# Four column tiles of 32 instead of two of 64 for the main products of a polysketch-attention and ELU kernel

## The chip, the core and the metric

The kernel runs on one core of a Trainium2 chip. The metric is the device time of one execution in microseconds (us). A core has a matrix engine (TensorE, PE in the profile, with its weight loads as PEld), a vector engine (VectorE, DVE), a scalar engine (ScalarE, ACT), GpSimd (POOL) and SyncE (SP), which here only issues DMAs. All arithmetic is float32.

## The reference

Polynomial-sketch attention over 4 batches, 4 heads, 1088 positions and head size 32 gives a matrix of 4352 tokens by 128; two dense layers with an ELU between them follow. The second part does nearly all the arithmetic.

```python
def phi(x):                              # r = 8, so 64 features
    a = np.einsum('rd,bhsd->bhsr', S1, x)
    b = np.einsum('rd,bhsd->bhsr', S2, x)
    return np.einsum('bhsi,bhsj->bhsij', a, b).reshape(*x.shape[:-1], r * r)
q_p, k_p = phi(q), phi(k)
kv  = np.einsum('bhsf,bhsd->bhfd', k_p, v);   z = np.sum(k_p, axis=2)
num = np.einsum('bhsf,bhfd->bhsd', q_p, kv)
den = np.einsum('bhsf,bhf->bhs', q_p, z)[..., None] + 1e-06
x   = (num / den).transpose(0, 2, 1, 3).reshape(4352, 128)
h   = x @ w_in                           # w_in 128 x 2048
g   = np.where(h > 0, h, np.exp(np.minimum(h, 0)) - 1)
out = g @ w_out                          # w_out 2048 x 128
```

## The kernel before

The tokens are cut into nine groups of the queries: groups 0 to 7 hold 512 tokens each, group 8 holds 256. The hidden size of 2048 is cut into eight pairs (`cp` = 0 to 7) of two 128-wide chunks (`c` = 0, 1). A step is one group and one pair, so there are 72 steps, listed in `steps`. All instructions are placed by hand in program order (a manual schedule). The main loop at the end of the kernel does, for step n: the first layer of step n (`mm1`), extra attention work that `at`, `mid` and `late` have hung on this step, the ELU of step n, and the second layer of step n-2.

- `mm1` computes h = w_in^T x for both chunks of the pair. `mm1_first` does the same for the very first step, with 256 columns at a time.
- The ELU is two ACT passes (lines 787 and 789) and one DVE pass (line 795, which writes the tile `gg`).
- The second layer has three forms. Groups 0 and 1 use `mm2`. Groups 2 to 7 use `mm2_seven`: the product of a pair with w_out is written as seven products of half size in the manner of Strassen, whose operand sums `tt` are made by POOL (lines 706 to 711) and whose weight sums are the tile `SS`. Group 8 uses `mm2_last`, with the hidden values as the stationary operand.
- Attention for the next groups runs between these. Per batch b, `KF` or `KF_late` makes the key features (line 303, line 322), `KA` (line 390, with `z_tile` on line 381) sums them with the values into `kv`, and `Z` and `KV` turn the sums by products with `SXh` and with an identity matrix. `q1` (line 538) and `q5` (line 644) make the query features and the attention output of a group. `q1_first`, `q1z_first`, `q1_second`, `q4_early` and `q5_early` do this for groups 0 and 1 in the prologue.

Every product with w_in and w_out and every turning product fills 128 output partitions from a contraction over 128 partitions. The stationary operand has 128 columns. The helper `halves` (line 225) cuts these into two column tiles of 64, each 128 partitions by 64 columns of the array, given by `tile_position`; `mm2_seven` (line 726) does it in its own loop, where the two tiles take the same 64 weight columns and different halves of the moving operand. Other products use other cuts: `KA` and `z_tile` use four column tiles of 128x32, `KF`, `q1_first`, `q1z_first` and `q1_second` two of 128x64, `KF_late` and `q5_early` tiles of 64x32, `q1` and `q5` tiles of 64x64 or 32x32. `keep_warm` and the transposes use the whole array. The profile prints the cut of a matrix instruction as rows*columns, for example 128*64.

One float32 matmul of the program shows in the trace as two weight loads (LDWEIGHTS) and two matmuls (MATMUL), called its two passes here.

Of the kernel before, what the change touches and what calls it, by code (L numbers as in the profile page):

```python
# [27 lines left out]
def kernel(  # L28
# [21 lines left out]
    nc = tc.nc  # L50
    B, H, S, D = q.shape
    R = S1.shape[0]
    P = 128
# [95 lines left out]
    W = const.tile([P, NP, 4 * P], F32, name="W")  # L149
# [50 lines left out]
    ident = const.tile([P, P], F32, name="ident")  # L200
# [19 lines left out]
    idle = psum.tile([P, 512], F32, name="idle", tag="o0", bufs=1)  # L220


    def halves(dst, lhs, rhs, **kw):
        for u in range(2):
            nc.tensor.matmul(dst[64 * u:64 * u + 64], lhs[:, 64 * u:64 * u + 64], rhs, skip_group_check=True,  # L225
                             tile_position=(0, 64 * u), **kw)

    def keep_warm(n, cols=256):
        for i in range(n):
# [16 lines left out]
    SXh = const.tile([P, FD], F32, name="SXh")  # L246
# [46 lines left out]
    kv_ps, kvz, feats, wzs, kf_ps = {}, {}, {}, {}, []  # L293
# [111 lines left out]

    def Z(b, ps, zl):

        halves(ps[:, 96:128], SXh[:], zl[:])

    def Z_out(b, ps):  # L410
        z = wzs[b] = SW[:, :, 2, :] if b == 0 else work.tile([FD, H, R], F32, name="wz", tag="wz")[:]
# [7 lines left out]

    def KV(b, ps):  # L420
        for f in range(2):
            halves(ps[:, 128 + P * f:128 + P * f + P], kvz[b][:, f].rearrange("p c s -> p (c s)"), ident[:])

    def KV_out(b, ps):
        if b in kvs:
# [8 lines left out]
    def Z_first():  # L434
        ps = psum.tile([P, 512], F32, name="zps", tag="h", bufs=4)
        for i in range(KT):
            z_tile(0, ps, i)
        return ps, ZC(0, ps)
# [7 lines left out]
    def KV_first():  # L446
        ps = psum.tile([P, 512], F32, name="kvps", tag="aux")
        KV(0, ps)
        KV_out(0, ps)
# [5 lines left out]
    abw, ans, qp, qpT, xg, xps = {}, {}, {}, {}, {}, {}  # L455
# [224 lines left out]
    hs, es, gs, ops = {}, {}, {}, {}  # L680
# [16 lines left out]
    def quarter(g, cp, c, y):  # L697
        return gs[g, cp][:, c].rearrange("p (u x s) -> p u x s", u=2, x=2)[:, :, y, :]
# [14 lines left out]
    def mm2_seven(g, cp, first, last):  # L713
        if first:
            acc[g] = [psum.tile([P, 512], F32, name="pa", tag="o0", bufs=1),
                      psum.tile([P, 512], F32, name="pb", tag="o1", bufs=1)]
        a, b = acc[g]
        t, w = ts.pop((g, cp)), [W[:, cp, 2 * P + 64 * i:2 * P + 64 * i + 64] for i in range(4)]
        b11, b21, b22 = quarter(g, cp, 0, 0), quarter(g, cp, 1, 0), quarter(g, cp, 1, 1)
        p1, p2, p6 = (a, 0, w[0], b11), (a, 1, w[2], b21), (a, 2, SS[:, 1, cp], t[:, 1])  # L720
        p4, p5 = (b, 0, w[3], t[:, 3]), (b, 1, SS[:, 0, cp], t[:, 0])
        p7, p3 = (b, 2, SS[:, 2, cp], t[:, 2]), (b, 3, SS[:, 3, cp], b22)
        todo = [p1, p2, p6, p3, p5, p7, p4] if first or last else [p1, p2, p3, p5, p7, p6, p4]
        for i, (bank, col, lhs, rhs) in enumerate(todo):
            for u in range(2):
                nc.tensor.matmul(bank[64 * u:64 * u + 64, P * col:P * col + P], lhs, rhs[:, u],  # L726
                                 start=(first and i in (0, 3)), stop=last, skip_group_check=True,
                                 tile_position=(0, 64 * u))
        del gs[g, cp]

    def fin_seven_copy(g):
# [34 lines left out]
    def mm1(g, cp, cs=(0, 1)):  # L766
        n = qn[g] * P
        if 0 in cs and (g, cp) not in hs:
            hs[g, cp] = [psum.tile([P, 512], F32, name="h", tag="h", bufs=4) for c in range(2)]
        for c in cs:  # L770
            halves(hs[g, cp][c][:, :n], W[:, cp, c * P:c * P + P], xg[g][:, :n])

    def mm1_first():
        hs[0, 0] = [psum.tile([P, 512], F32, name="h", tag="h", bufs=4) for c in range(2)]
        for w in range(2):
            for c in range(2):
                cols = [x[:].rearrange("p (m w s) -> p w m s", w=2, s=P)[:, w] for x in (hs[0, 0][c], xg[0])]
                halves(cols[0], W[:, 0, c * P:c * P + P], cols[1])

    def elu_a(g, cp, c, parts=(0, 1)):  # L780

# [20 lines left out]
    def mm2(g, cp, first, last):  # L802
        n = qn[g] * P
        if first:
            ops[g] = psum.tile([P, 512], F32, name="o", tag=f"o{g % 2}", bufs=1)
        gg = gs.pop((g, cp))
        for c in range(2):
            halves(ops[g][:, :n], W[:, cp, (2 + c) * P:(3 + c) * P], gg[:, c, :n],
                   start=(first and c == 0), stop=(last and c == 1))

    def fin1(g):
# [12 lines left out]
    def mm2_last(cp, first, last):  # L824
        g = NQ - 1
        if first:
            ops[g] = [psum.tile([P, P], F32, name="ol", tag=t, bufs=k) for t, k in (("o0", 1), ("aux", 2))]
        gg = gs.pop((g, cp))
        for a in range(4):
            c, i = (a % 2, a // 2) if last else divmod(a, 2)  # L830
            halves(ops[g][i][:], gg[:, c, i * P:i * P + P], W[:, cp, (2 + c) * P:(3 + c) * P],
                   start=(first and c == 0), stop=(last and c == 1))

    def fin_last():
# [14 lines left out]
    zps, zl = Z_first()  # L849
    q1_first()  # L850
    KO_pool()
    KO_first(4, 5)
    KO_first(5, 7)
    Z(0, zps, zl)
    Z_out(0, zps)
    KO_first(7, KT)
# [14 lines left out]
    q5_early(0)  # L871
    q1_second()
    mm1_first()
    RA(2)
    RB(2)
    RC(1)
    elu_a(0, 0, 0)
    elu_a(0, 0, 1)
    mm1(0, 1)
    q2(1, 2)  # L880
    q4_early(1)
# [4 lines left out]
    elu_d(0, 0, 1)  # L886
    q5_early(1)
    mm2(0, 0, True, False)
    RC(3)
    for c in range(2):  # L890
# [40 lines left out]
    def turn(b):  # L931
        Z(b, kv_ps[b], zls.pop(b))
        KV(b, kv_ps[b])
# [59 lines left out]
    for n in range(2, N + 2):  # L993
        if n < N:
            g, cp = steps[n]
            mm1(g, cp)
        for f, *a in extra.get(n, ()):
            f(*a)
        if n < N:
            elu(g, cp, 0)  # L1000
            if seven(g):
                sums7(g, cp, 0)
            for f, *a in extra.get((n, 0), ()):
                f(*a)
            before = steps[n - 2]
            ends = n > 3 and seven(before[0]) and before[1] == NP - 1
            if ends:
                elu_a(g, cp, 1, (0,))
                mm2_seven(*before, False, True)
                fin_seven_copy(before[0])  # L1010
                elu_a(g, cp, 1, (1,))
                fin_seven_a(before[0])
                elu_d(g, cp, 1)
            else:
                elu(g, cp, 1)
            if seven(g):
                sums7(g, cp, 1)
            if ends:
                fin_seven_b(before[0])
        for f, *a in extra.get((n, 1), ()):  # L1020
            f(*a)
        g, cp = steps[n - 2]
        if g == NQ - 1:
            mm2_last(cp, cp == 0, cp == NP - 1)
        elif seven(g):
            if cp < NP - 1:
                mm2_seven(g, cp, cp == 0, False)
        elif n > 2:
            mm2(g, cp, cp == 0, cp == NP - 1)
            if cp == NP - 1:  # L1030
                fin1(g)
# [30 lines left out]
```

## Time and profile before

| | |
|---|---|
| median of 5 runs | 267.39 us (267.13 to 267.83) |
| the profiled execution: its own time | 267.83 us |
| the profiled execution: its span | 266.0 us |
| PE busy | 260.0 us, 3113 matmul records |
| PEld busy | 154.9 us, 3113 weight-load records |
| DVE / ACT / POOL busy | 187.9 / 184.1 / 159.9 us |
| granted TensorE clock | 1.00 in every window looked at |

How to read it: "L225" is line 225 of the kernel. A group row gives line, engine, operation, out<-in, the cut and the moving size, the number of records, then busy time and mean duration of one. Records of PE overlap each other, because matmuls are pipelined and because several tiles run at once. The pace of PE is therefore read from the times between starts, not from durations. A row of the timeline merges neighbouring records of one kind: start in us, extent from the first start to the last end in us, then what they are, and how many.

### The profile page before, as it was taken

The page shows a single profiled execution, that of the slowest core. Times are in us where ns is not written, and L with a number is a line of the kernel's source. Part 1 is how long each engine was busy: PE and PEld are TensorE (multiplying, and loading weights), DVE is VectorE, ACT ScalarE, POOL GpSimd, SP SyncE. Part 2 cuts the span into 40 slices and gives each one's busy share as a digit, 9 for nine tenths or more (in the row PEclk, how much of TensorE's full clock was granted, in tenths as well). Part 3 has the DMA queues.
Part 4 walks back from the last instruction along what each step waited for, and adds up shares of the span by engine and source line. Part 5 has one row for each costly group of instructions (what it writes and reads, how often), then busy time and mean ns, then how long its engine had stood idle before and what let it go on. Part 6 is the DMA issues. An engine that isn't in the chain of part 4 may idle for free.

```text
span 266.0 us, 7682 instructions
## 1 busy us (share of the span) xinstructions
PE 260.0 (98%) x3113; PEld 154.9 (58%) x3113; DVE 187.9 (71%) x347; ACT 184.1 (69%) x355; POOL 159.9 (60%) x233
## 2 busy tenths in 40 slices
PE   8899999999999999999999999999999999999994
PEld 7743323343334665668566666666766666667884
DVE  7799999996969796996657766554346444673652
ACT  2479978677566565786577777777777777777782
POOL 4400008203405985798858799898688888898300
PEclk9999999999999999999999999999999999999999
DMA  5998960011002300001100110001000100010011
GB/s 186 321 348 240 283 174 10 0 40 48 0 0 35 50 4 0 2 2 18 27 5 0 21 22 2 0 12 27 9 0 15 28 4 0 14 18 13 2 30 32
DMA packets 26402, 13.60 MB, mean 51 GB/s; under 512 B 19200, under 2 KB 24576, under 8 KB 26368
## 3 DMA queue, kind: packets, MB, share of 16 engines
q1 hardware_dynamic: 25920, 12.79, 18.7%
q8 instruction: 24, 0.39, 0.6%
q10 hardware_dynamic: 448, 0.33, 0.4%
q14 instruction: 10, 0.08, 0.1%
HBM read 10.88 MB, written 2.23 MB: 49 GB/s over the span
## 4 chain that ended last, share of the span: by engine, by line
PE 93%; DVE 5%; issue 1%; ACT 0%; DVEq 0%
PE h L225 43%; PE pb L726 16%; PE pa L726 12%; PE o L225 11%; PE ol L225 3%; PE kv L390 1%; PE idle L230 1%; PE h L644 1%; PE qps L644 1%; PE abp L303 1%; DVE qp L582 1%; PE kfps L322 1%; PE qps L538 1%; PE kv L225 1%; DVE raw L121 1%
## 5 line engine op out<-in xcount | busy, mean ns | idle before, releaser
L795 DVE SCALAR_TENSOR_TENSOR gg<-e,h 128x512 f32<-128x512 f32 (+1 forms) x144 | 92.2, 652 | 64.1 <-ACT e L789 62.8
L225 PE MATMUL h<-xg,W 128*64 128x512 f32 (+1 forms) x584 | 128.9, 563 | 0.0
L787 ACT ACTIVATE e<-h 128x512 f32<-128x512 f32 (+1 forms) x144 | 81.5, 566 | 50.5 <-PE h L225 46.7
L789 ACT ACTIVATE e<-e 128x512 f32<-128x512 f32 (+1 forms) x144 | 87.5, 607 | 4.4
L225 PEld LDWEIGHTS h<-xg,W 128*64 128x64 f32 x584 | 40.2, 137 | 47.4 <-issue 37.3
L706 POOL TENSOR_TENSOR tt<-gg 128x256 f32<-128x256 f32 x48 | 35.2, 733 | 16.3 <-DVE gg L795 15.9
L709 POOL TENSOR_TENSOR tt<-gg 128x256 f32<-128x256 f32 x48 | 35.5, 739 | 14.1 <-DVE gg L795 13.8
L711 POOL TENSOR_TENSOR tt<-gg,tt 128x256 f32<-128x256 f32 x48 | 36.6, 762 | 3.8
L710 POOL TENSOR_TENSOR tt<-tt,gg 128x256 f32<-128x256 f32 x48 | 35.2, 734 | 3.8
L726 PEld LDWEIGHTS pa<-gg,W 128*64 128x64 f32 x384 | 23.6, 137 | 22.8 <-issue 22.0
L225 PE MATMUL o<-gg,W 128*64 128x512 f32 x128 | 30.5, 597 | 0.4 <-DVE W L129 0.4
L726 PE MATMUL pa<-gg,W 128*64 128x128 f32 x384 | 29.5, 274 | 0.0
L726 PE MATMUL pb<-tt,SS 128*64 128x128 f32 x384 | 29.1, 273 | 0.0
L726 PEld LDWEIGHTS pb<-tt,SS 128*64 128x64 f32 x384 | 22.6, 137 | 0.0
L126 POOL TENSOR_TENSOR raw<-raw,tiny 128x512 f32<-128x512 f32 x1 | 1.0, 1042 | 30.0 <-DVE raw L121 30.0
L726 PE MATMUL pb<-gg,SS 128*64 128x128 f32 x192 | 18.7, 273 | 0.0
L726 PE MATMUL pb<-tt,W 128*64 128x128 f32 x192 | 18.6, 273 | 0.0
L726 PE MATMUL pa<-tt,SS 128*64 128x128 f32 x192 | 18.6, 273 | 0.0
L225 PEld LDWEIGHTS o<-gg,W 128*64 128x64 f32 x128 | 8.5, 136 | 16.2 <-issue 13.8
L726 PEld LDWEIGHTS pa<-tt,SS 128*64 128x64 f32 x192 | 12.1, 137 | 0.0
L726 PEld LDWEIGHTS pb<-tt,W 128*64 128x64 f32 x192 | 12.1, 137 | 0.0
L726 PEld LDWEIGHTS pb<-gg,SS 128*64 128x64 f32 x192 | 12.1, 137 | 0.0
(150 smaller groups left out, 244.6 us busy)
## 6 DMA issues: line engine op xcount, KB each, us to landing
raw<-in_moe_w_in_dram SPq DMA_DIRECT2D x8, 256.0 KB, 6.5
raw<-in_moe_w_out_dram SPq DMA_DIRECT2D x8, 256.0 KB, 6.6
hd_k<-in_k_dram SPq DMA_DIRECT2D x3, 544.0 KB, 8.0
hd_q<-in_q_dram SPq DMA_DIRECT2D x3, 544.0 KB, 8.2
v<-in_v_dram SPq DMA_DIRECT2D x4, 288.0 KB, 7.6
out_dram<-ob SPq DMA_DIRECT2D x72, 16.0 KB, 1.5
v<-in_v_dram SPq DMA_DIRECT2D x4, 256.0 KB, 6.9
out_dram<-ob SPq DMA_DIRECT2D x16, 32.0 KB, 1.6
```

What stands on the lines that cost most here:

```text
L121: nc.vector.scalar_tensor_tensor(lo.bitcast(F32), lo, 2.0 ** -32, raw[:, :, 1], op0=MUL, op1=ADD)
L225: nc.tensor.matmul(dst[64 * u:64 * u + 64], lhs[:, 64 * u:64 * u + 64], rhs, skip_group_check=True, tile_position=(0, 64 * u), **kw)
L230: nc.tensor.matmul(idle[:, :cols], some[:, :P], some[:, :cols], skip_group_check=True)
L644: nc.tensor.matmul(ps[w][s * r:s * r + s, 64 * k:64 * (k + m)], lhs, qpT[g, i][rows, o + 2 * k:o + 2 * (k + m), f, :], start=(f == 0 and j ...
L706: nc.gpsimd.tensor_tensor(t[:, 0], b12, b11, op=SUB)
L709: nc.gpsimd.tensor_tensor(t[:, 2], b22, b12, op=SUB)
L710: nc.gpsimd.tensor_tensor(t[:, 1], t[:, 2], b11, op=ADD)
L711: nc.gpsimd.tensor_tensor(t[:, 3], b21, t[:, 1], op=SUB)
L726: nc.tensor.matmul(bank[64 * u:64 * u + 64, P * col:P * col + P], lhs, rhs[:, u], start=(first and i in (0, 3)), stop=last, skip_group_che ...
L787: nc.scalar.activation(e, hs[g, cp][c][:, :n], RELU, scale=-1.0)
L789: nc.scalar.activation(e, e, EXP, scale=-1.0)
L795: nc.vector.scalar_tensor_tensor(gs[g, cp][:, c, :n], es[g, cp][:, c, :n], -1.0, hs[g, cp][c][:, :n], op0=ADD, op1=MAX)
```

## The change

`halves` becomes `quarters`: four matmuls, one for each column tile of 32. All six callers follow it (`Z`, `KV`, `mm1`, `mm1_first`, `mm2`, `mm2_last`). The loop of `mm2_seven` gains an inner loop, so that each of its half-width products is cut in two again. Nothing else is edited: the same values are multiplied, into the same banks, in the same order of products. In the changed kernel the line of `quarters` is again 225, and the matmul of `mm2_seven` is on line 728.

```diff
-    def halves(dst, lhs, rhs, **kw):
-        for u in range(2):
-            nc.tensor.matmul(dst[64 * u:64 * u + 64], lhs[:, 64 * u:64 * u + 64], rhs, skip_group_check=True,
-                             tile_position=(0, 64 * u), **kw)
+    def quarters(dst, lhs, rhs, **kw):
+        for c in range(4):
+            nc.tensor.matmul(dst[32 * c:32 * c + 32], lhs[:, 32 * c:32 * c + 32], rhs, skip_group_check=True,
+                             tile_position=(0, 32 * c), **kw)
...
     def Z(b, ps, zl):
-        halves(ps[:, 96:128], SXh[:], zl[:])
+        quarters(ps[:, 96:128], SXh[:], zl[:])
...
     def mm2_seven(g, cp, first, last):
...
             for u in range(2):
-                nc.tensor.matmul(bank[64 * u:64 * u + 64, P * col:P * col + P], lhs, rhs[:, u],
-                                 start=(first and i in (0, 3)), stop=last, skip_group_check=True,
-                                 tile_position=(0, 64 * u))
+                for w in range(2):
+                    r = 64 * u + 32 * w
+                    nc.tensor.matmul(bank[r:r + 32, P * col:P * col + P], lhs[:, 32 * w:32 * w + 32], rhs[:, u],
+                                     start=(first and i in (0, 3)), stop=last, skip_group_check=True,
+                                     tile_position=(0, r))
...
     def mm1(g, cp, cs=(0, 1)):
...
-            halves(hs[g, cp][c][:, :n], W[:, cp, c * P:c * P + P], xg[g][:, :n])
+            quarters(hs[g, cp][c][:, :n], W[:, cp, c * P:c * P + P], xg[g][:, :n])
```

`KV`, `mm1_first`, `mm2` and `mm2_last` change in the same way, by the name of the helper alone.

More of the change, by code (lines that the diff above doesn't have):

```diff
@@ L421, in KV @@
         for f in range(2):
-            halves(ps[:, 128 + P * f:128 + P * f + P], kvz[b][:, f].rearrange("p c s -> p (c s)"), ident[:])
+            quarters(ps[:, 128 + P * f:128 + P * f + P], kvz[b][:, f].rearrange("p c s -> p (c s)"), ident[:])
     def KV_out(b, ps):
@@ L777, in mm1_first @@
                 cols = [x[:].rearrange("p (m w s) -> p w m s", w=2, s=P)[:, w] for x in (hs[0, 0][c], xg[0])]
-                halves(cols[0], W[:, 0, c * P:c * P + P], cols[1])
+                quarters(cols[0], W[:, 0, c * P:c * P + P], cols[1])
     def elu_a(g, cp, c, parts=(0, 1)):
@@ L807, in mm2 @@
         for c in range(2):
-            halves(ops[g][:, :n], W[:, cp, (2 + c) * P:(3 + c) * P], gg[:, c, :n],
+            quarters(ops[g][:, :n], W[:, cp, (2 + c) * P:(3 + c) * P], gg[:, c, :n],
                    start=(first and c == 0), stop=(last and c == 1))
@@ L830, in mm2_last @@
             c, i = (a % 2, a // 2) if last else divmod(a, 2)
-            halves(ops[g][i][:], gg[:, c, i * P:i * P + P], W[:, cp, (2 + c) * P:(3 + c) * P],
+            quarters(ops[g][i][:], gg[:, c, i * P:i * P + P], W[:, cp, (2 + c) * P:(3 + c) * P],
                    start=(first and c == 0), stop=(last and c == 1))
```

## The prediction

> **What bounds the kernel now.** I read the page first: the busy row, the clock row, the queues and the chain that ended last.
>
> ```profile
> PE 260.0 (98%) x3113; PEld 154.9 (58%) x3113; DVE 187.9 (71%) x347; ACT 184.1 (69%) x355; POOL 159.9 (60%) x233
> ...
> PEclk9999999999999999999999999999999999999999
> ...
> q8 instruction: 24, 0.39, 0.6%
> ...
> PE 93%; DVE 5%; issue 1%; ACT 0%; DVEq 0%
> ```
>
> PE carries 93% of the chain, at full clock. Busy PE alone is no proof of a bound, so the second view is PE's timeline of one whole step with seven products, which gives the pace between starts.
>
> ```profile
> 200.85 0.61 PE L726 MATMUL pa<-gg,W 128*64 128x128 f32 x8
> 201.29 0.39 PE L726 MATMUL pa<-tt,SS 128*64 128x128 f32 x4
> 201.51 0.39 PE L726 MATMUL pb<-gg,SS 128*64 128x128 f32 x4
> 201.73 0.61 PE L726 MATMUL pb<-tt,SS 128*64 128x128 f32 x8
> 202.16 0.39 PE L726 MATMUL pb<-tt,W 128*64 128x128 f32 x4
> 202.38 1.89 PE L225 MATMUL h<-xg,W 128*64 128x512 f32 x8
> 204.10 0.61 PE L726 MATMUL pa<-gg,W 128*64 128x128 f32 x8
> ```
>
> From 200.85 to 202.38 there are 28 records of 128 columns in 1.53 us. They start in pairs, one for each column tile, so 14 pairs take 109 ns each. From 202.38 to 204.10 four pairs of 512 columns take 1.72 us, 430 ns each. Both fit 0.833 ns a column plus 2.5 ns. The next step begins with no gap. From 22.3 us to the last matmul at 262.4 us the matrix engine streams like this; what interrupts it is almost only a change of the tile cut. Thus the pace of a pass, and the price of a change of cut, are the two things by which this edit can move the end.
>
> **The change part by part.**
>
> *1. The passes.* A pass over all 128 output columns is now four records instead of two, each reading the same moving columns. From the records of the groups I count the old pairs: 316 of 512 columns (504 and 128 records), 40 of 256 (80), 848 of 128 (1536 of line 726, 128 of `mm2_last`, 32 of `KV`), 8 of 32; 1212 in all. Every nanosecond that a pass of four costs beyond a pass of two is 1.2 us. The trace holds the same form already: `KA` runs four 128*32 tiles at once. The clearest is batch 0, which starts behind a wait, with nothing queued.
>
> ```profile
> 10.19 1.21 PE L390 MATMUL kv<-kp,v 128*32 128x64 f32 x72
> ```
>
> A record here lasts 0.22 us, so the last starts at 11.18: 72 records, 18 passes of four, in about 1.0 us. In the single records every fourth start is 55 or 56 ns after the one four before. By the pace above 64 columns take 53.3 + 2.5 = 55.8 ns. Four tiles therefore stream as fast as two, and I take 0 for this part. `KF_late` (64*32, eight tiles, 288 columns, below) gives the same for long streams: its first-to-second pass takes 267 ns against 242.5, and the 25 ns are the load at entry (part 3). From these rows the error is within 0.1 ns a pass either way, so -0.1 to +0.1 us.
>
> *2. Issue and weight loads.* PE's instructions grow from 6226 to 6226 + 2 x 2424 = 11074. With seven products a step is 2 x 4 x 2 x 2 = 32 instructions for `mm1` and 7 x 4 x 2 x 2 = 112 for the second layer; 144 in 3.25 us. The tightest place is the 112 in 1.53 us, 13.6 ns each. In batch 0's `KA` 144 instructions went through in 1.0 us, 7 ns each, from an empty queue. That also means four loads of 32 columns in 56 ns, where 109 are to be had. I take 0.
>
> The Trainium skill speaks against this step. "TensorEngine Tiling (Array Packing)", under Instruction Overhead, says "Each matmul has ~60 cycle overhead on TRN2" and warns against cutting what is already small. "TensorE: Matmul & The Clock Gate", under "Wait — 56ns, not 53.3ns?", has a floor of about 25 ns between starts, or about 62 ns for each MATMUL when decode runs in the sequencer's code. Four times 25 is 100 ns and still fits into 109; four times 62 is 248, which over 848 passes of 128 columns would be 848 x (248 - 109) = 118 us more, an estimate from that page. The row decides: `KA` starts a matmul every 14 ns, under either floor, so neither holds between tiles here.
>
> *3. Changes of cut.* Before, `KA` stands between products of 128*64.
>
> ```profile
> 117.79 1.89 PE L225 MATMUL h<-xg,W 128*64 128x512 f32 x8
> 119.61 0.32 PE L390 MATMUL kv<-kp,v 128*32 128x64 f32 x8
> ...
> 120.80 0.22 PE L390 MATMUL kv<-kp,v 128*32 128x64 f32 x1
> 120.94 0.66 PE L726 MATMUL pa<-gg,W 128*64 128x128 f32 x8
> 121.43 0.39 PE L726 MATMUL pb<-gg,SS 128*64 128x128 f32 x4
> ```
>
> The four pairs of `h` end their stream at 117.79 + 4 x 0.43 = 119.51; `KA` starts at 119.61, 0.10 late. `KA` ends its stream at 120.80 + 0.05 = 120.85; the next begins at 120.94, 0.09 late, and its first eight records take 0.49 instead of 0.44 us. That is 0.10 + 0.09 + 0.05 = 0.24 us, and the three late batches (56.3, 88.8, 119.6 us) show the same. After the change all neighbours are 128*32, as `KA` and `z_tile` are between themselves, where no such gap stands. So 3 x 0.24 = 0.72 us are removed.
>
> The other changes of cut stay, for example into `KF_late`:
>
> ```profile
> 36.54 1.46 PE L225 MATMUL h<-xg,W 128*64 128x512 f32 x6
> 37.93 0.72 PE L322 MATMUL kfps<-kT,Sxp 64*32 64x288 f32 x16
> 38.57 0.65 PE L225 MATMUL o<-gg,W 128*64 128x512 f32 x2
> ```
>
> Again 0.10 us at the exit (36.54 + 3 x 0.43 = 37.83), and at the return a first pass of 0.65 instead of 0.60. This 0.05 is the weight load that nothing hides; with 32 columns it is about 0.025 (`KA` and `KF_late` show 24 and 25 ns). Nine returns behind 22.3 us give -0.23 us. At the nine exits a pass of four ends later than one of two by two offsets of about 6.7 ns: +0.12 us. Together -0.11.
>
> *4. The prologue.* Here the change adds changes of cut.
>
> ```profile
> 8.25 0.69 PE L478 MATMUL abqp<-Sab,qT 128*64 128x64 f32 x16
> 8.77 0.26 PE L225 MATMUL zps<-zl,SXh 128*64 128x32 f32 x4
> 8.96 0.46 PE L230 MATMUL idle<-some 128*128 128x96 f32 x2
> ...
> 9.14 0.19 DVE L412 TENSOR_TENSOR SW<-zps,bmask 128x32 f32<-128x32 f32 x1 [0.42 <-PE zps L225]
> ```
>
> `Z` follows `q1_first` without a gap and will be about 0.1 us late. DVE waits for it, and behind that wait are queued `KO_first`, the rounding of the weights and `q2_den`, a DVE chain without slack that the chain view follows to 22.3 us. So +0.11 us reach the end (0 to 0.2). The other new one, `q1_second` (128*64) before `mm1_first`, makes h later by about 0.1 us. The ACT passes finish at 19.67 and DVE takes up `gg` at 20.01, so 0.34 us cover it; without that cover it costs 0.1.
>
> *5. The rest.* Waits, their places and their number on PE, ACT, DVE and POOL stay as they are; queues of SP and POOL are untouched. Once PE is earlier, ACT and DVE could become late. Setting each second-layer product against the end of its last `gg`, I find at least 1.4 us behind the first step, so 0.7 us saved is not eaten. Four moving streams could slow the other engines' reads. Under `KA`, ACT's 583 ns stands against a median of 589, DVE's 690 against 686, POOL's 740 against 733: nothing, or 1% at most, with that slack over it.
>
> Sum: 0 + 0 - 0.72 - 0.11 + 0.11 = -0.72 us. The profiled execution took 267.83 us (span 266.0), so it would be 267.1; the median is 0.44 below that execution, which gives 266.7 us.
>
> **The rivals.**
>
> *Slower: issue becomes the bound in the seven products.* Place: lines 726/728, 85 to 250 us, 48 steps. It decides from the point where an instruction takes over 13.6 ns for long. At 15 ns, 112 would take 1.68 us instead of 1.53, and 48 x 0.15 = 7 us more, 274. What speaks for it: `KA`'s burst is 144 instructions long, while here it is tens of thousands of bytes of program. The instruction queue moved 24 packets for 0.39 MB; 4848 more instructions at the same 63 bytes are 0.31 MB, about 19 packets, and every one that is not fetched ahead shows whole, some 1.1 us as now (0.6% of 16 engines over 266 us, by 24); all 19 exposed are 21 us, 288. Against it: in 3.25 us only 144 instructions are needed, and 256 of them (one packet) last 5.8 us.
>
> *No change within 0.2%.* The 0.1 us gaps may belong to `KA`'s own start and end rather than to the change of cut, or `KA`'s uneven tiles (the sums of z go round the tiles) leave holes that the neighbours do not fill. Then -0.1 + 0.1 is left, 267.4. Against it: `KF_late` shows the same 0.10 at another cut.
>
> *More gain.* `KA` takes 1.24 us from its first start to its last stream's end, where the fullest tile has 18 x 55.8 + 6 x 29.2 = 1.18 us of work. If the neighbours fill its uneven ends too, 3 x 0.06 = 0.2 us more, 266.5, and 266.3 if the prologue loses nothing.
>
> That the change does not do what it says is excluded: the order of instructions shows four 32-wide matmuls for each two.
>
> **How the numbers follow.** The forecast gets 0.60 with the gain's variant in it, no change 0.14, slower 0.26. The forecast's own range is 265.9 to 267.3, with the bounds of parts 1, 3 and 4. 0.2% of 267.39 is 0.53 us, about what a measurement of this kernel can tell from no change, so the forecast is faster in about 0.85 of its cases: 0.51. Same is 0.60 x 0.15 + 0.14 = 0.23. Slower is 0.26, spread from 268 up to 288, about a third of it under 269.5. With 265.8 to 269.5 some 0.17 lies above and 0.02 below.
>
> **What would show it.** Right: every stretch of line 225 and 728 at 109 and 430 ns for each four records; no gap around `KA`, and it flows into its neighbours; 43 packets of the instruction queue; first passes after a change of cut longer by 25 instead of 50 ns; `SW` on line 412 later by 0.1 us. Wrong: passes of 128 columns at over 109 ns for four (issue or a start offset that adds up), or PE idle put down to "issue" at intervals of some 256 instructions (fetch), or the gap around `KA` as before.

## The result and the profile after

| | before | changed |
|---|---|---|
| first measurement, median (lowest to highest, runs) | 267.61 us (267.07 to 269.66, 51) | 267.03 us (266.30 to 267.72, 30) |
| first measurement, ratio | | 0.9976, interval 0.9967 to 0.9985 |
| second measurement, ratio | | 1.0006, interval 0.9994 to 1.0017 |
| third measurement, ratio | | 1.0000, interval 0.9988 to 1.0013 |
| profiled execution: time, span | 267.83 us, 266.0 us | 267.05 us, 265.3 us |

A ratio weighs all runs of a measurement, so it need not be the ratio of the medians; of the runs of this document one of before (271.38 us) and two of the kernel with 64 columns below (295.11 and 295.96 us) were in a slower state and are left out of the ratios.

The forecast was 266.7 us, 0.26% under the 267.39 us that it started from. The first measurement gives a gain of 0.24%, close to it. The second and the third, each against before on its own chip, show none; whether the chips differ in this was not tested. All three are told here because the difference between them turned out to be the point of the case: the matrix engine's stream became about 1 us shorter (239.08 to 239.43 us in three traces, 240.10 to 240.44 us in three of before, one of them with the pads told of below), and the end of the kernel gave back a part of it that changes from run to run.

The page of the changed kernel, the busy row, the clock, the instruction queue and the chain:

```profile
PE 258.1 (97%) x5345; PEld 151.0 (57%) x5345; DVE 187.7 (71%) x347; ACT 184.0 (69%) x355; POOL 160.4 (60%) x233
...
PEclk9999999999999999999999999999999999999999
...
q8 instruction: 42, 0.69, 1.1%
...
PE 93%; DVE 5%; issue 1%; ACT 0%; DVEq 0%
```

The same engine bounds the kernel at the same clock. PE has 5345 records instead of 3113, and the instruction queue moves 42 packets instead of 24. Such a packet is a DMA transfer of 16 KB (0.69 MB in 42) that brings the next piece of PE's program. PE's timeline of one step with seven products:

```profile
200.75 1.90 PE L225 MATMUL h<-xg,W 128*32 128x512 f32 x16
202.47 0.62 PE L728 MATMUL pa<-gg,W 128*32 128x128 f32 x16
202.91 0.40 PE L728 MATMUL pb<-gg,SS 128*32 128x128 f32 x8
203.12 0.62 PE L728 MATMUL pb<-tt,SS 128*32 128x128 f32 x16
203.56 0.40 PE L728 MATMUL pa<-tt,SS 128*32 128x128 f32 x8
203.78 0.40 PE L728 MATMUL pb<-tt,W 128*32 128x128 f32 x8
204.00 1.90 PE L225 MATMUL h<-xg,W 128*32 128x512 f32 x16
```

The counts have doubled, the distances between starts have not changed: 1.72 us for the first layer (202.47 - 200.75) and 1.53 us for the seven products (204.00 - 202.47), as before. The timeline around `KA`, with its rows in the middle left out:

```profile
116.48 1.90 PE L225 MATMUL h<-xg,W 128*32 128x512 f32 x16
118.19 0.29 PE L390 MATMUL kv<-kp,v 128*32 128x64 f32 x8
...
119.36 0.27 PE L728 MATMUL pa<-gg,W 128*32 128x128 f32 x1
119.36 0.22 PE L390 MATMUL kv<-kp,v 128*32 128x64 f32 x1
119.39 0.63 PE L728 MATMUL pa<-gg,W 128*32 128x128 f32 x15
119.79 0.44 PE L728 MATMUL pb<-gg,SS 128*32 128x128 f32 x8
```

The stream of `h` ends at 116.48 + 1.72 = 118.20 and `KA` begins at 118.19, with no gap. At the other end the first record of line 728 starts beside the last one of `KA`, at 119.36: the two run into each other. A change of cut that stayed, into `KF_late`:

```profile
35.52 1.90 PE L225 MATMUL h<-xg,W 128*32 128x512 f32 x16
37.35 0.72 PE L322 MATMUL kfps<-kT,Sxp 64*32 64x288 f32 x16
37.99 1.50 PE L225 MATMUL o<-gg,W 128*32 128x512 f32 x12
```

It is still there: 35.52 + 1.72 = 37.24, so `KF_late` starts 0.11 us late. In the prologue, PE and then DVE:

```profile
8.02 0.46 PE L478 MATMUL abqp<-Sab,qT 128*64 128x64 f32 x10
8.41 0.27 PE L225 MATMUL zps<-zl,SXh 128*32 128x32 f32 x8
8.61 0.46 PE L230 MATMUL idle<-some 128*128 128x96 f32 x2
```

```profile
8.82 0.19 DVE L412 TENSOR_TENSOR SW<-zps,bmask 128x32 f32<-128x32 f32 x1 [0.55 <-PE zps L225]
```

DVE now waits 0.55 us for `Z` instead of 0.42. What the prediction did not look at is the other end. SP's timeline shows the output stores (here "the stores of group 7" are the 16 of `ob`, "the last stores" the two of `ol`); the extent runs from the first issue to the end of the last. First before, then changed:

```profile
252.42 8.49 SPq L763 DMA_DIRECT2D out_dram<-ob  x16
262.34 1.19 SPq L842 DMA_DIRECT2D out_dram<-ol  x2
```

```profile
250.81 9.77 SPq L765 DMA_DIRECT2D out_dram<-ob  x16
260.73 2.38 SPq L844 DMA_DIRECT2D out_dram<-ol  x2
```

The two last stores of SP took 2.38 us to issue instead of 1.19, and behind them the kernel ends. From the single records of the two profiled executions:

| us | before | changed | difference |
|---|---|---|---|
| start of the stream (first `mm2`) | 22.33 | 21.73 | -0.60 |
| stream, to the end of the last matmul | 240.11 | 239.08 | -1.03 |
| tail, to the end of the span | 3.60 | 4.45 | +0.85 |

The first row is largely chance, not the edit: already the first `z_tile` product, which stands ahead of everything that was edited on PE, starts at 7.64 us in one and at 7.19 us in the other. "Stream" and "tail" are used in this sense below.

### The profile page after: what moved, and what is told of

Its sections match the earlier page's. It is cut to its first block, busy times and chain, and to the rows that moved or that the text cites. A ratio compares the mean times of both kernels' runs of the same rounds, so it can differ in the third digit from the quotient of the medians.

```text
span 265.3 us, 12146 instructions
## 1 busy us (share of the span) xinstructions
PE 258.1 (97%) x5345; PEld 151.0 (57%) x5345; DVE 187.7 (71%) x347; ACT 184.0 (69%) x355; POOL 160.4 (60%) x233
## 4 chain that ended last, share of the span: by engine, by line
PE 93%; DVE 5%; issue 1%; ACT 0%; DVEq 0%
PE h L225 43%; PE pb L728 16%; PE pa L728 12%; PE o L225 11%; PE ol L225 3%; PE kv L390 1%; PE idle L230 1%; PE h L644 1%; PE qps L644 1%; DVE qp L582 1%; PE kfps L322 1%; PE qps L538 1%; PE abp L303 1%; PE kv L225 1%; DVE raw L121 1%
## 5 line engine op out<-in xcount | busy, mean ns | idle before, releaser
L225 PE MATMUL h<-xg,W 128*32 128x512 f32 (+1 forms) x1168 | 130.0, 563 | 0.0
L225 PEld LDWEIGHTS h<-xg,W 128*32 128x32 f32 x1168 | 38.1, 110 | 49.1 <-issue 39.6
L706 POOL TENSOR_TENSOR tt<-gg 128x256 f32<-128x256 f32 x48 | 35.3, 736 | 15.8 <-DVE gg L797 15.4
L728 PEld LDWEIGHTS pa<-gg,W 128*32 128x32 f32 x768 | 22.6, 110 | 23.5 <-issue 22.9
L225 PE MATMUL o<-gg,W 128*32 128x512 f32 x256 | 30.6, 594 | 0.3 <-DVE W L129 0.3
L728 PE MATMUL pa<-gg,W 128*32 128x128 f32 x768 | 30.2, 273 | 0.0
L728 PE MATMUL pb<-tt,SS 128*32 128x128 f32 x768 | 30.1, 273 | 0.0
L728 PEld LDWEIGHTS pb<-tt,SS 128*32 128x32 f32 x768 | 22.2, 110 | 0.0
L728 PE MATMUL pb<-tt,W 128*32 128x128 f32 x384 | 19.6, 273 | 0.0
L728 PE MATMUL pb<-gg,SS 128*32 128x128 f32 x384 | 19.6, 273 | 0.0
L728 PE MATMUL pa<-tt,SS 128*32 128x128 f32 x384 | 19.6, 273 | 0.0
```

Source lines behind the costliest of these rows:

```text
L225: nc.tensor.matmul(dst[32 * c:32 * c + 32], lhs[:, 32 * c:32 * c + 32], rhs, skip_group_check=True, tile_position=(0, 32 * c), **kw)
L706: nc.gpsimd.tensor_tensor(t[:, 0], b12, b11, op=SUB)
L728: nc.tensor.matmul(bank[r:r + 32, P * col:P * col + P], lhs[:, 32 * w:32 * w + 32], rhs[:, u], start=(first and i in (0, 3)), stop=last, s ...
```

## Experiments

The theory after the comparison had three parts: passes cost nothing; the stream gains where cuts no longer change; and the doubled instruction stream brings packets that can delay SP's stores at the end. Rivals were that the gain lies elsewhere than in the changes of cut, that instruction issue is nearly exhausted, and that the tail grew by chance and not by packets.

**The helper alone.** Everything of the change except `mm2_seven`, which returns to two tiles. Now each of the 48 steps has two changes of cut.

```diff
-                for w in range(2):
-                    r = 64 * u + 32 * w
-                    nc.tensor.matmul(bank[r:r + 32, ...], lhs[:, 32 * w:32 * w + 32], rhs[:, u], ...
+                nc.tensor.matmul(bank[64 * u:64 * u + 64, ...], lhs, rhs[:, u], ...
```

> The helper uses four tiles of 128x32, the seven products stay at two of 128x64, so 48 steps change the cut twice each. Theory (the gain came from changes of cut that fell away around KA, and a pass itself costs the same): each pair of changes costs about 0.10 + 0.03 + 0.11 + 0.05 us minus nothing, 0.25 to 0.3 us a step, so 12 to 14 us slower than the changed kernel, 279 to 281 us, with 109 and 430 ns a pass everywhere. Rival (the gaps belong to KA's own start and end, or to something that KA waits for): no gap between mm1 and the seven products, 267 us.

Measured: 279.61 us, ratio 1.045 (1.0433 to 1.0466), stream 252.18 us. PE's timeline of one step:

```profile
199.59 1.92 PE L225 MATMUL h<-xg,W 128*32 128x512 f32 x16
201.44 0.66 PE L726 MATMUL pa<-gg,W 128*64 128x128 f32 x8
...
202.80 0.39 PE L726 MATMUL pb<-tt,W 128*64 128x128 f32 x4
203.12 1.92 PE L225 MATMUL h<-xg,W 128*32 128x512 f32 x16
204.97 0.66 PE L726 MATMUL pa<-gg,W 128*64 128x128 f32 x8
```

A step takes 203.12 - 199.59 = 3.53 us instead of 3.25. Against the changed kernel the stream is 13.1 us longer; by 48 steps that is 0.273 us for a pair of changes, and it can be read in the rows: 201.44 stands 0.13 us behind 199.59 + 1.72, where four passes end (0.10 of drain, 0.03 of loads that nothing hides), and the first eight records take 0.66 instead of 0.61. So a change of cut has a price of its own, here shown 48 times, and it needs no `KA`. The rival that the gap belongs to `KA`'s own start and end falls.

**Moving the packets, early.** Fourteen tiny matmuls behind batch 0's `KA`, so that every later packet is asked for 56 of PE's instructions (14 matmuls of two loads and two passes) earlier in the program's work.

```diff
+    def pad(n):
+        for i in range(n):
+            c = 32 * (i % 4)
+            nc.tensor.matmul(idle[c:c + 32, :16], some[:, :32], some[:, :16], skip_group_check=True,
+                             tile_position=(0, c))
...
     KA(0)
+    pad(14)
```

> The changed kernel with 14 tiny matmuls (16 columns, 128x32 tiles, results unused) behind KA of batch 0, where PE waits for ACT: 56 more PE instructions. Theory (the last packet of the PE instruction queue, at 260.83 us, holds up the last two stores on SP by about 0.9 us, and it comes when PE has read a fixed number of its instructions): the packet comes about 1 us earlier, among the stores of group 7, the last stores take 0.55 us each again, the tail behind the last matmul falls from 4.4 to 3.6 us, and the time by 0.5 to 0.9 us to about 266.3. Rival (the long last stores are chance, or come from the stores of group 7 before them): time as the changed kernel, 267.0, tail about as often long as short.

Measured: 267.75 us, ratio 1.0008 (0.9997 to 1.0019). The last packet came at 261.06 us, and the last matmul ended at 262.37. SP's timeline:

```profile
252.38 8.69 SPq L771 DMA_DIRECT2D out_dram<-ob  x16
262.29 1.19 SPq L850 DMA_DIRECT2D out_dram<-ol  x2
```

The packet now lay between the stores of group 7 and the last ones, those took 1.19 us again, and the tail was 3.59 us. That supports the packets. The time did not fall, though. The pads brought a cost of their own: PE stood for 0.81 us until 15.47 us (the profile names ACT as the cause; the next kernel tells more), and the stream began 14.89 us behind the first `z_tile` product instead of 14.54. The stream itself was longer too, 239.51 us, for a reason not found.

**The counterpart in the kernel before.** Eighteen pads at the same place in before, meant to give it one more packet at the end.

> The kernel before with 18 such tiny matmuls in the same place: 72 more PE instructions, so that one more packet of the PE instruction queue should come within about 0.6 us of the last matmul. Theory of the packet: the last stores on SP take 1.0 to 1.8 us instead of 0.55, the tail grows from 3.6 to about 4.5 us, the time by 0.5 to 0.9 us to about 268.2. Rival: tail and time as before, 267.5.

Measured: 270.66 us, ratio 1.0112 (1.0093 to 1.013), and the expectation missed. There was no further packet (24; the last at 256.13 us), and the tail stayed at 3.58 us. The 3 us lie ahead of the stream, which began 17.50 us behind the first `z_tile` product instead of 14.69. They begin with one wait of PE:

```profile
PE qtp L600 <- issue: 1.7, 1, 1.7
```

```profile
12.35 1.10 PE L600 MATMUL qtp<-ident,qp 128*128 128x128 f32 x6
15.20 0.44 PE L600 MATMUL qtp<-ident,qp 128*128 128x128 f32 x2 [1.74 <-issue]
```

In the middle of a run of equal transposes PE stops for 1.74 us and waits for no other engine. The stop lies at PE's instruction number 449, and so did that of the kernel with fourteen pads. The packet for what follows started at 12.66 us and ended at 13.82, and PE went on at 15.2 us. In the kernel before, the same instruction number is reached at about 15.3 to 15.5 us, without a stop. The pads did not add work worth 1.7 us; they brought PE to the edge of an instruction block before it was there. How the 1.7 us grow to 2.8 by the start of the stream was not followed. So this run says nothing about the tail, but it shows that PE can outrun its instructions.

**How fast instructions can come.** Each of the seven products cut in two once more, by 64 moving columns: 224 instead of 112 instructions in the same 1.53 us of work.

```diff
-                    nc.tensor.matmul(bank[r:r + 32, P * col:P * col + P], lhs[...], rhs[:, u], ...
+            for x in (0, 64):
+                ...
+                    nc.tensor.matmul(bank[r:r + 32, P * col + x:P * col + x + 64], lhs[...], rhs[:, u, x:x + 64], ...
```

> The changed kernel with each product of the seven cut again in the moving direction, two times 64 columns: 28 passes of four tiles a step instead of 14, and 256 PE instructions a step instead of 144, one every 7 ns in the seven. Theory (PE takes an instruction every 7 ns for as long as it must): a pass of 64 columns costs 56 ns, 28 x 55.8 = 1.562 instead of 1.528 us, 0.034 us a step over 48 steps, 1.6 us more, 268.5 us, with more stores held up by packets. Rival (issue or fetching binds for long streams, from about 10 ns an instruction): 224 x 10 ns = 2.24 us for the seven, 0.7 us a step, 34 us more; at 13.6 ns 73 us more.

Measured: 290.39 and 290.71 us, ratio 1.0857 (1.0832 to 1.0881); stream 262.96 us. The page's queue row, PE's waits, and its timeline:

```profile
q8 instruction: 62, 1.02, 1.4%
```

```profile
PE pb L728 <- issue: 8.0, 13, 1.5
PE pa L728 <- issue: 3.8, 11, 0.9
```

```profile
214.03 0.44 PE L728 MATMUL pb<-tt,SS 128*32 128x64 f32 x17
214.99 0.36 PE L728 MATMUL pb<-tt,SS 128*32 128x64 f32 x11 [0.52 <-issue]
```

Between the stops a pass of four keeps its 55.9 ns, 7 ns an instruction, as in batch 0's `KA`. But PE stops, for 0.2 to 1.5 us, and the 26 stops from 90 us on stand multiples of 256 instructions apart (to within four). A step of this kernel has 32 + 224 = 256 instructions, one block, and became 23.9 / 48 = 0.50 us longer: 3.25 + 0.50 = 3.75 us for a block, about 14.6 ns an instruction on average. That is the supply in the main loop, as far as this run shows it; it is an average, since not every block began with a stop. The changed kernel uses a block in 256 / 144 x 3.25 = 5.8 us, so it has room by a factor of 1.5. The claim that an instruction comes every 7 ns for as long as it must falls: it holds within a block.

**The changed kernel again.** The same kernel, unedited, twice more.

> The changed kernel once more, as the partner of the next three on the same chip. By the trace of it on hand: about 0.6 us below the kernel before, 43 or 42 packets of the instruction queue with the last one within 0.5 us of the last matmul, a tail of 4.4 us.

> The changed kernel once more as the partner of the next two. If the last packet of the instruction queue comes in some executions just before the end and in others not at all, the times spread over 1.2 us or more, with a median between 266.5 and 267.5; the kernel before spreads over about 0.7 us.

Measured: 267.5 us, ratio 1.0006 (0.9994 to 1.0017), and 267.38 us, ratio 1.0000 (0.9988 to 1.0013). Streams 239.31 and 239.43 us, tails 3.61 and 3.89 us. SP's timeline of the third trace:

```profile
251.87 10.46 SPq L765 DMA_DIRECT2D out_dram<-ob  x16
262.43 1.19 SPq L844 DMA_DIRECT2D out_dram<-ol  x2
```

Here the last two stores are undisturbed, but the sixteen before them took 10.46 us instead of 8.49, because two of them met a packet (2.05 us at 252.23, 1.81 us at 257.18), and SP reached the last ones 0.57 us behind the last matmul. In the second, the last packet had come at 256.60 us, the queue caught up, and the tail was as short as that of before. One kernel, three tails.

A second loss lies behind the span, where no tail shows it. The time of a run is a little more than its span: by 1.74 to 1.87 us in the 97 runs of before that were taken beside these kernels. In the changed kernel it is over 1.95 us in 22 of 65 runs, up to 2.86, and 0.1 to 0.2 us more than in before on average. The third trace is of such a run: 268.21 us with a span of 265.8, and a packet of the instruction queue at 266.99 us, behind the end of the span. In the changed kernels below whose last packet comes earlier, by pads or by fewer instructions, and in the one above with fourteen pads, none of 60 runs is over 1.89. That fits a packet behind the end, but one trace with it is no proof.

**Moving the packets, late.** The same pads, but placed ahead of the first `mm2`, behind the prologue: fourteen in the changed kernel, twenty-two in before.

```diff
+    pad(14)          # 22 in the kernel before
     mm2(0, 0, True, False)
```

> The changed kernel with the 14 tiny matmuls (results unused) behind q5_early of group 1, where PE waits about 0.34 us for DVE, and behind the block boundary at instruction 449 that stalled the padded prologues. Theory (the last packet of the instruction queue holds up the last stores; its place is a count of PE instructions): last packet 1 to 1.5 us before the last matmul, last stores 0.55 us each, tail 3.6 us, stream at most 0.2 us longer, so 0.5 to 0.9 us under the changed kernel. Rival (tail is chance): as the changed kernel, or 0.1 us more for the added matmuls.

> The kernel before with 22 tiny matmuls in that same later place, 88 PE instructions more: a 25th packet of the instruction queue should start within about 0.7 us of the last matmul. Theory of the packet: the last stores on SP take 1.0 to 1.8 us, tail 4.4 instead of 3.6 us, and with 0.2 us for the added matmuls 0.7 to 1.2 us above the kernel before, about 268.5. Rival (the tail is a property of the four-tile stream, not of the packet): tail 3.6 us, 0.2 us above the kernel before. If no 25th packet comes, it tells nothing.

Measured: the changed kernel with pads 266.99 us, ratio 0.9996 (0.9981 to 1.001), stream 239.13 us; before with pads 267.59 us, ratio 1.0014 (0.9998 to 1.003), stream 240.10 us. The stop in the prologue was gone, as expected. The tails were 4.31 and 3.73 us, where 3.6 and 4.4 had been expected: both missed. SP's timeline of the first:

```profile
251.32 10.86 SPq L771 DMA_DIRECT2D out_dram<-ob  x16
262.28 1.20 SPq L850 DMA_DIRECT2D out_dram<-ol  x2
```

The packet, moved to 260.25 us, left the last stores alone and met the last but one of group 7 (1.65 us at 260.05). SP issues in order, so the last stores started 0.97 us behind the last matmul. In before with pads the 25th packet came at 261.64 us, together with the first of the last stores, which took its usual 0.55 us; only the second was longer, 0.70. So it isn't enough that a packet falls into the end; what it costs depends on the moment, here between 0.1 and 0.9 us.

**Pads and the prologue.** Sixteen pads, and batch 0's `Z` in two tiles of 64 again.

```diff
     def Z(b, ps, zl):
-        quarters(ps[:, 96:128], SXh[:], zl[:])
+        if b:
+            quarters(ps[:, 96:128], SXh[:], zl[:])
+            return
+        for u in range(2):
+            nc.tensor.matmul(ps[64 * u:64 * u + 64, 96:128], SXh[:, 64 * u:64 * u + 64], zl[:],
+                             skip_group_check=True, tile_position=(0, 64 * u))
...
+    pad(16)
     mm2(0, 0, True, False)
```

> As the last one with 16 tiny matmuls, and Z of batch 0 back in two tiles of 64, which takes the change of cut behind q1_first away. Theory: Z starts without a gap again, SW on line 412's successor is 0.1 us nearer to q1_first, tail 3.6 us; 0 to 0.1 us under the last one. Rival: the prologue is bound by the rounding of the weights on DVE and their loads, and the 0.1 us is lost there: no difference.

Measured: 267.19 us, ratio 0.9994 (0.9985 to 1.0004), stream 239.08 us, tail 4.24 us: the packet at 260.42 us met the last store of group 7 (1.81 us). Nudging the packets is no cure, since an end of some ten microseconds, with eighteen stores close together, and a packet every 4 to 5 us leave few free places.

**Fewer packets at the end.** From the last query stage on (step 62, at about 238 us) the products return to two tiles; the place is chosen because the cut changes there anyway.

```diff
+    cut = [32]
     def quarters(dst, lhs, rhs, **kw):
-        for c in range(4):
-            nc.tensor.matmul(dst[32 * c:32 * c + 32], lhs[:, 32 * c:32 * c + 32], rhs, skip_group_check=True,
-                             tile_position=(0, 32 * c), **kw)
+        s = cut[0]
+        for c in range(0, P, s):
+            nc.tensor.matmul(dst[c:c + s], lhs[:, c:c + s], rhs, skip_group_check=True,
+                             tile_position=(0, c), **kw)
...
-                for w in range(2):
-                    r = 64 * u + 32 * w
+                for w in range(0, 64, cut[0]):
+                    r, s = 64 * u + w, cut[0]
...
         for f, *a in extra.get(n, ()):
             f(*a)
+        if n == 62:
+            cut[0] = 64
```

> The changed kernel, but from the last query stage on (step 62, at 238 us) all products go back to two tiles of 64. The cut changes there anyway, so no change of cut is added; PE's instructions in the last 22 us are halved, and the last packet should come about 5 us before the end, among the stores of group 7, with a gap behind them. Theory (the gain of the stream is 1.0 us, and packets near the end take 0 to 0.9 us of it back through SP's stores): stream as long as the changed kernel's within 0.05 us, tail 3.6 us in the profile, 0.8 to 1.1 us under the kernel before, ratio 0.996 to 0.997, and at or under the changed kernel on the same chip. Rival (the changed kernel's mixed result comes from the prologue): as the changed kernel, ratio 0.998 to 1.001.

Measured: 266.78 us (266.4 to 267.11, 7 runs), ratio 0.9972 (0.9961 to 0.9982). Stream 239.02 us, as in the changed kernel; the last packet at 254.88 us; tail 3.54 us. SP's timeline:

```profile
251.65 8.38 SPq L768 DMA_DIRECT2D out_dram<-ob  x16
261.56 1.28 SPq L847 DMA_DIRECT2D out_dram<-ol  x2
```

Some 0.7 us of the stream's gain of 1.0 us now arrive, where the changed kernel, measured beside it on the same chip, showed no gain. So the loss lay in the doubled instruction stream at the end of the kernel. That it works through packets which hold up SP's stores, and perhaps through one behind the span, is read from the rows and not shown by this experiment alone.

**Four tiles in the middle only.** As the last one, and the prologue in two tiles as well.

```diff
-    cut = [32]
+    cut = [64]
...
+    cut[0] = 32
     mm2(0, 0, True, False)
```

> As the last one, with the prologue too in two tiles of 64, so that four tiles of 32 run only from the first second-layer product (22 us) to the last query stage (238 us). Both ends of that stretch meet another cut anyway. Theory: prologue free of the two added changes of cut, from the first z to the first h 0.2 us shorter than in the changed kernel; stream and tail as in the last one; 0 to 0.2 us under it. Rival (DVE's rounding chain and the loads bound the prologue, so that 0.2 us on PE are not seen at its end): same time as the last one.

Measured: 266.30 us (265.94 to 266.48, 5 runs), ratio 0.9953 (0.9941 to 0.9965). Beside it on the same chip the changed kernel took 266.63 to 268.38 us and before 267.07 to 267.97, so this version beats both. PE's timeline at the end of the four-tile stretch, and SP's at the end:

```profile
236.57 1.90 PE L228 MATMUL h<-xg,W 128*32 128x512 f32 x16
238.40 0.67 PE L647 MATMUL qps<-qpT,kvq 64*64 64x128 f32 x16
239.00 0.66 PE L731 MATMUL pa<-gg,W 128*64 128x128 f32 x8
```

```profile
250.93 8.49 SPq L768 DMA_DIRECT2D out_dram<-ob  x16
260.84 1.19 SPq L847 DMA_DIRECT2D out_dram<-ol  x2
```

SP's two rows are those of before again (8.49 and 1.19 us), though PE ends 1.5 us earlier than there. The query stage takes up the return to two tiles. `SW` starts 1.51 us behind the first `z_tile` product, where all kernels with `Z` in four tiles take 1.63 or 1.64 and before takes 1.50.

**Before, once more.** A second profile of the kernel before.

> A second profile of the kernel before, to tell what of its prologue and tail repeats. Theory: from the first z to SW 1.50 us again (1.63 in every four-tile prologue), stream from the first second-layer product to the last matmul 240.1 us again, tail 3.6 us. If the prologue up to that first product takes 14.5 us instead of 14.7, the shorter prologue of the changed kernel's first trace was chance.

Measured: 267.64 us, stream 240.44 us, tail 3.59 us, `SW` 1.50 us behind the first `z_tile` product. From that product to the start of the stream it took 14.39 us, where the first profile has 14.69 and the profiles of the changed kernel have 14.53 to 14.55. The two executions of one kernel thus differ by 0.30 us, more than the cost that was looked for. Their rows tell where. Up to 15.8 us DVE's chain keeps the same distances in both; then three passes in a row of the first profile are slow:

```profile
15.82 0.38 DVE L117 TENSOR_SCALAR raw<-raw 128x256 uint32<-128x256 uint32 x1
16.23 0.56 DVE L121 SCALAR_TENSOR_TENSOR raw<-raw 128x256 f32<-128x256 uint32 x1
16.82 0.52 DVE L129 SCALAR_TENSOR_TENSOR W<-raw,W 128x256 f32<-128x256 f32 x1
```

In the second profile, and in that of the changed kernel, they take 0.29 or 0.30, 0.43, and 0.42 or 0.43 us. With these 0.31 us set aside, the first profile agrees with the second. The kernel with four tiles in the middle only took 14.38 us, so two tiles in the prologue give 14.38 or 14.39 and four give 14.53 to 14.59 (five traces without pads; a sixth, of the kernel with 64 columns, had waited 1.1 us for a load and took 14.93).

Put together, with the gap between the end of the last matmul and the issue of the first of the two last stores (below zero, where the store waits for an earlier matmul only):

| kernel | stream, us | last packet, us | store behind last matmul, us | tail, us |
|---|---|---|---|---|
| before | 240.11 | 255.59 | -0.10 | 3.60 |
| before again | 240.44 | 255.51 | -0.10 | 3.59 |
| before, 22 pads late | 240.10 | 261.64 | -0.10 | 3.73 |
| changed, first | 239.08 | 260.83 | -0.08 (and 2.38 long) | 4.45 |
| changed, second | 239.31 | 256.60 | -0.08 | 3.61 |
| changed, third | 239.43 | 257.22, next at 266.99, behind the span | +0.57 | 3.89 |
| changed, 14 pads late | 239.13 | 260.25 | +0.97 | 4.31 |
| changed, 16 pads, `Z` in two | 239.08 | 260.42 | +0.91 | 4.24 |
| two tiles at the end | 239.02 | 254.88 | -0.10 | 3.54 |
| four tiles in the middle only | 239.39 | 256.24 | -0.10 | 3.58 |

## Why the prediction was right or wrong, point by point

**Passes (part 1): right.** A pass of four takes 109 and 430 ns, in every stretch looked at. The sum rested on a wrong count: line 726 has 1344 records (48 steps of 28), not the 1536 that the prediction counted, so the passes are 1116 in all and 752 of 128 columns, PE's instructions grow to 2 x 5345 = 10690, and 42 packets were to be expected, not 43. As the cost of a pass is zero, nothing in the time follows from it; the prediction's estimate of 118 us, which uses the same count, would have been 752 x 139 ns = 105 us.

**Issue and loads (part 2): right for this kernel, wrong as a rule.** The step "144 instructions went through in 1.0 us, 7 ns each", taken for a lasting rate, is one that failed: it is a rate within a block. Over blocks the kernel with 64 columns got 14.6 ns. The slower rival was therefore nearer than the prediction thought. Its point of decision, 13.6 ns for long, was put on the wrong length, though: the block of 256 decides, and over a block the changed kernel needs an instruction every 5.8 us / 256 = 22.6 ns. Its own argument against the rival, 256 instructions in 5.8 us, was the one that held.

**Changes of cut (part 3): right mechanism, too small a term.** Stretches of equal work, from a product of `h` before each late `KA` to behind it, became shorter by 0.35, 0.35 and 0.31 us: 1.01 us, where 0.72 was predicted. The "more gain" variant, in which the neighbours fill `KA`'s uneven ends, gives 0.92, and the rows at 119.36 us show them doing so. Taken apart, around `KA` itself 0.33 us went each time. `Z` and `KV`, which follow, became 0.05 us shorter each time, a term that the sum did not have. And the unevenness of the tiles is carried on (the four starts of a pass of `h` lie 0.06 to 0.11 us apart instead of 0.02) to the next change of cut, where 0.03, 0.03 and 0.08 us of the gain are lost again. The stretches with a change of cut that stayed became shorter by 0.013 to 0.015 us each, against a predicted (0.23 - 0.12) / 9 = 0.012. One was longer by 0.026. The whole stream gained 1.03 us in the first pair of profiles; the streams of before lie at 240.10 to 240.44 and those of the changed kernel, with and without pads late, at 239.08 to 239.43. The helper alone shows the price without `KA`.

**Prologue (part 4): right.** `SW` is 0.13 us later in every prologue with `Z` in four tiles, against 0.11 predicted, and DVE's chain without slack carries the delay on: the stream starts 0.15 us later (14.53 to 14.59 us behind the first `z_tile` product instead of 14.38 or 14.39). In the first pair of profiles the three slow passes of before hid it. The other new change of cut, ahead of `mm1_first`, makes the first `h` 0.10 us later behind `q1_second` (0.81 us instead of 0.71) and was covered, as predicted. The version with the prologue in two tiles is faster than the one without by 0.48 us in the medians (266.30 against 266.78). The prologue accounts for 0.21 us of that in the traces (14.38 against 14.59); what the rest is stays open, and the two ranges touch (265.94 to 266.48 and 266.4 to 267.11).

**The rest (part 5): the step that failed.** "Queues of SP and POOL are untouched" is true of the instructions and false of the time. The prediction itself had counted 19 more packets of the instruction queue, but weighed them only as a danger to PE. They get in the way of the stores. In the single records from 60 us on, every store whose issue took over 0.9 us overlaps a packet: 9 of 9 in before, 15 of 15 in the changed kernel, and none of the 126 and 119 stores without a packet was so long. In the middle of the kernel no engine waits for a store. At the end, SP is a queue of eighteen stores, 0.48 us apart, and what delays one of group 7 delays the last two. With four packets behind 245 us instead of two, the chance of a hit there is larger, and the loss of 0 to 0.85 us, with up to 1 us more behind the span in single runs, stands against a gain of 1.03. The sum had no such term. That the first measurement met the forecast's time is in part luck: the stream gained 0.2 us more than the sum said, and the end took about as much back. In the other two measurements nothing of the gain was left; the one trace of each (tails of 3.61 and 3.89 us) can't tell how the loss is spread over their runs.

The rivals: no change by a gap that is `KA`'s own is refuted by the helper alone; no change in the time did occur, from another cause. More gain is what the stream did. The slower rival's mechanism exists, as the kernel with 64 columns shows; the changed kernel stays clear of it by a factor of 1.5.

## What to carry to other kernels

Cutting a product into more column tiles costs the stream nothing as long as a block of 256 PE instructions lasts clearly longer than their supply (3.75 us on average in the kernel with 64 columns), and it pays where it spares changes of cut, of which a pair cost 0.27 us. But more instructions are also more DMA packets: look at which transfers stand where the kernel ends, and use the longer form only where it saves something. A gain of 0.2 to 0.4% needs the tail looked at by itself, in more than one profile, before the stream's gain is believed.

## What the runs showed of the hardware

- PE takes its program in blocks of 256 instructions (42 packets for 10690, 62 for 16066), and stops lie multiples of 256 instructions apart in the kernel with 64 columns, and at the same instruction in the two kernels with early pads. When PE gets to the edge too early it stops and the profile says "issue": 1.74 us in the transposes of the prologue, 0.2 to 1.5 us in the kernel with 64 columns. In that prologue other loads were running, and PE went on only 1.4 us after the packet had ended.
- A store's issue on SP takes 0.43 us and 1.0 to 2.1 us when it meets a packet of the instruction queue, which lasts 0.9 to 1.6 us. Not every packet that overlaps a store does this: 3 of 12 such stores in before and 4 of 19 in the changed kernel took 0.44 us or less. Why the 25th packet of before with pads cost only 0.13 us, when that of the changed kernel, 0.10 us behind the issue of the same store, cost 0.85, stays open.
- A change of cut takes 0.10 us at the exit from tiles that run evenly, and up to 0.20 us where they do not (the first attention product behind the last late `KA` in the changed kernel); the entry adds 0.05 us with loads of 64 columns and 0.03 with loads of 32.
- Also open: why the stream of one kernel differs by up to 0.35 us between two executions, why three DVE passes of one prologue took 0.31 us longer than in the others, and whether the loss behind the span is that of a packet.
